# Reordering the start of an attention and feed-forward kernel: V of the first batch loaded after Q and K, and both heads of a pair normalised in one pass

## The chip, the cores and the metric

The kernel runs on one core of one Trainium2 chip. The metric is device time in microseconds (us) of that core; lower is better. Each kernel is executed several times in rounds that alternate with the kernel before. All numbers below are medians, and the profiles are of single executions, so a profiled span can differ from a median. Every run lists the granted clock of TensorE as a share of full speed. A run is labelled fast or slow; for one core, slow means over 1.5% above the fastest run of the same kernel.

A ratio in this document is the mean time of one kernel's fast runs over the mean of the other kernel's fast runs in the same rounds, with a 95% interval. It is therefore not quite the ratio of the medians that I quote beside it.

## The reference

There are 8 batches of 8 heads, 576 positions by 64. Blocks of 64 positions attend to themselves and to what lies before them. The result is laid out as 4608 rows of 512 and goes through a feed-forward layer. The shapes matter: every input is float32 in DRAM, and the kernel works in bf16.

```python
def _attn_ref(q, k, v):                      # 8 x 8 x 576 x 64
    scores = np.matmul(q, k.transpose(0, 1, 3, 2)) / np.sqrt(D)
    mask = (pos[:, None] // 64) >= (pos[None, :] // 64)
    scores = np.where(mask, scores, -1e9)
    ...                                      # softmax over the last axis
    return np.matmul(attn, v)

def _moe_ref(x, w_in, w_out, beta):          # x 4608x512, w_in 512x2048, w_out 2048x512
    h = x @ w_in
    g = h * (1.0 / (1.0 + np.exp(-beta * h)))
    return g @ w_out
```

## The kernel before

A unit is one pair of heads of one batch: four units to a batch, 32 in all. A unit loads Q and K, casts and transposes them, multiplies the scores in four groups, takes the exponentials on ScalarE (ACT), multiplies by V (with a column of ones, which gives the sum of each row), divides by that sum on VectorE (DVE), and transposes the result into xT. The feed-forward layer multiplies xT by w_in, applies its activation (the result is gT) and multiplies gT by w_out. It works on row chunks of 512 rows. Chunk 0 needs batch 0, and chunk 1 needs batch 1.

The program records operations with estimated durations in a plan. A list scheduler then fixes the order of every engine when the kernel is built. Each engine runs its list strictly in that order, and semaphores make it wait where an operand is not there yet. So an operation with a late operand also holds up those behind it on its engine. That property matters below.

The parts that the argument touches are the loads, and what each waits for. Q, K and most V loads are issued by the sync engine (SP), the first half of batch 0's V by ACT, and the weights by GpSimd (POOL):

```python
for a in range(4):                                   # w_in in four pieces of 512 columns
    win.append(P.op("POOL", 1000, fwi, xfer=4200, dma=(f"d_win{a}", 1), prio=-19))
for a in range(4):                                   # w_out likewise
    wout.append(P.op("POOL", 1000, fwo, xfer=4200, dma=(f"d_wout{a}", 1), prio=-18))
...
vs.append(P.op("ACT" if (b, h0) == (0, 0) else "SP", ...))   # loads of V
...
for w in win:
    w.deps += [ld["Q", 1], ld["K", 1]]
for w in wout:
    w.deps += [ld["Q", 6], ld["K", 6]]
for u in range(4, 8):                                # batch 1 waits for the second piece of w_in
    for o in [ld["Q", u], ld["K", u]] + (ld["V", 1, 0] if u == 4 else []):
        o.deps += [win[1]]
```

In PSUM, the memory into which TensorE writes its results, used here as eight banks, score groups take a pair of banks out of (0,1) and (2,3). Everything else, the V product too, takes single banks, mostly from 4 to 7. Two such banks serve one V product, and each head is normalised by itself:

```python
pa, pb = P.tile("P1"), P.tile("P1")
...
for w, p in enumerate((pa, pb)):                     # head 0, head 1
    r = P.op("DVE", 180, fr, deps=[av], tiles=[p, ti], prio=0)               # reciprocal, 128x5
    m = P.op("DVE", dve_t(320), fm, deps=[av, r], tiles=[p, ti, tx], prio=0) # multiply, 128x320
```

Finally there are fillers: multiplies of two constant matrices that nobody reads, which the scheduler puts where TensorE has nothing to do at the start, to keep its clock up.

The softmax here doesn't subtract the row's maximum and nothing guards it: scores larger than these inputs give would overflow.

Of the kernel before, what the change touches and what calls it, by code (L numbers as in the profile page):

```python
# [21 lines left out]
class Tile:  # L22


    def __init__(self, cls):
        self.cls, self.slot, self.left, self.users = cls, None, 0, []

# [16 lines left out]
class Plan:  # L44
# [29 lines left out]
    def schedule(self):  # L74
# [23 lines left out]
        def can(o):  # L98
            nb = {}
            for t in o.tiles:  # L100
                if t.slot is None:
                    nb[t.cls] = nb.get(t.cls, 0) + 1
            for c, n in nb.items():
                if c == "PP":
                    if sum(1 for a in (0, 2) if a in banks and a + 1 in banks) < n:
                        return False
                elif c == "P1":
                    ok = [k for k in banks if k >= 4 or pairs == 0]
                    if len(ok) < n:
                        return False  # L110
                elif len(free[c]) < n:
                    return False
            return True

        fill = [o for o in self.ops if o.fill]
        while nsched < len(self.ops) - len(fill) or pend:
# [25 lines left out]
            while progress:  # L142
                progress = False
                for e in engs:
# [4 lines left out]
                    for o in pool:  # L149
# [10 lines left out]
                        if o.fill and (now > o.fill or mode == "row"):  # L160
                            continue
# [16 lines left out]
                    for t in o.tiles:  # L178
                        if t.slot is None:
                            if t.cls == "PP":  # L180
                                a = next(a for a in (0, 2) if a in banks and a + 1 in banks)
                                banks.remove(a)
                                banks.remove(a + 1)
                                t.slot = a
                                o.deps += bank_last[a] + bank_last[a + 1]
                                pairs -= 1
                            elif t.cls == "P1":
                                ok = [k for k in banks if k >= 4 or pairs == 0]
                                t.slot = ok[0]
                                banks.remove(t.slot)  # L190
                                o.deps += bank_last[t.slot]
                            else:
                                t.slot = free[t.cls].pop(0)
                                o.deps += last[(t.cls, t.slot)]
# [90 lines left out]
def bass_blockwise_causal_attn__then__act_swish_beta_kernel(  # L285
# [10 lines left out]
    with es:  # L296
# [29 lines left out]
        ost = [sb(f"ost{i}", [128, DM], f32) for i in range(3)]  # L326
        PS = es.enter_context(nc.psum_tensor("PS", [128, 8, 512], f32))
# [19 lines left out]
        def pr(u):  # L347
            b, c = divmod(u, NPAIR)
            return 10 * u if b < 2 else 994 + 100 * (b - LAG) + 4.9 * c
# [12 lines left out]
        c2.same, c4.same = [c1], [c3]  # L362
        ones, vzero = [], []
# [11 lines left out]
        for i in range(NQ, NE):  # L375
# [12 lines left out]
        szero = [P.op("POOL", 350, mk(lambda g, i=i: g.memset(ST[i][64:128, 4, :, :], 0.0)), prio=-3)  # L388
                 for i in range(NS)]
# [3 lines left out]
        for a in range(4):  # L393
            def fwi(g, e, a=a):
                n = slice(512 * a, 512 * a + 512)
                return [g.dma_start(w_in[:, :, n], moe_w_in[:, n].rearrange("(c p) n -> p c n", p=128))]

            win.append(P.op("POOL", 1000, fwi, xfer=4200, dma=(f"d_win{a}", 1), prio=-19))
        for a in range(4):
            def fwo(g, e, a=a):  # L400
                return [g.dma_start(w_out[:, 4 * a:4 * a + 4, :],
                                    moe_w_out[512 * a:512 * a + 512, :].rearrange("(j p) n -> p j n", p=128))]

            wout.append(P.op("POOL", 1000, fwo, xfer=4200, dma=(f"d_wout{a}", 1), prio=-18))


        for i in range(NFILL):
# [5 lines left out]
            o = P.op("PE", 110, ff, deps=[c2, c4], tiles=[tf], lat=280, mode="full", prio=1e6)  # L413
# [5 lines left out]
        for b in range(B):  # L419
            ts, t = P.tile("Vs"), P.tile("V")  # L420
            tl[b] = t
            for h0, h1 in ([(0, 4), (4, 8)] if b == 0 else [(0, 8)]):
                vs = []
                for i in range(6):
                    def fv(g, e, ts=ts, b=b, h0=h0, h1=h1, i=i):
                        if i < 4:
# [7 lines left out]
                    vs.append(P.op("ACT" if (b, h0) == (0, 0) else "SP", 300 + 550 * n, fv, tiles=[ts],  # L434
                                   xfer=1400 * n, prio=(-50 if h0 == 0 else 3.5) if b == 0 else 4 * b + (3.5 if b < 2 else 0.5),
# [4 lines left out]
                def fw(g, e, ts=ts, t=t, h0=h0, h1=h1):  # L440
# [3 lines left out]
                         prio=4 * b + 0.5 - 30 * (b < 1))  # L444
                for h in range(h0, h1, 2):
                    load[4 * b + h // 2] = o

# [14 lines left out]
        for u in range(NU):  # L462
# [8 lines left out]
            if b < QB:  # L471

                turned = []
                for w, (nm, src) in enumerate((("Q", q), ("K", k))):
# [8 lines left out]
                    def fn(g, e, ts=ts, tn=tn, p=p, w=w):  # L483
# [3 lines left out]
                    onp = b == 1 or w == 1  # L487
                    o = P.op("POOL" if onp else "DVE", 850 if onp else 470, fn, deps=[o], tiles=[ts, tn],
                             prio=-26 + u if onp else -1)
# [14 lines left out]
                    turned.append(P.op("DVE", dve_t(576), fc, deps=[o], tiles=[pt, tt_], prio=0))  # L504
# [33 lines left out]
            for g0 in range(4):  # L538
# [17 lines left out]
                o = P.op("PE", 220 if g0 < 3 else 60, fq, deps=cps, tiles=[ps, tqk, te],  # L556
# [30 lines left out]
            pa, pb = P.tile("P1"), P.tile("P1")  # L587
            ti, tx = P.tile("inv"), P.tile("xq")

            def fav(g, e, te=te, pa=pa, pb=pb, Tv=Tv, c=c):  # L590
                for h in range(2):
                    for i in range(5):
                        for t in range(i + 1):
                            o = PS[:, (pa if h == 0 else pb).slot, 65 * i:65 * i + 65]
# [3 lines left out]

            av = P.op("PE", 30 * 34, fav, deps=ex + zs + [load[u]], tiles=[te, Tv, pa, pb, ti, tx],
                      lat=30 * 34 + 180, mode="full", prio=pr(u)+.4)  # L600
            nrm = []
            for w, p in enumerate((pa, pb)):
                def fr(g, e, w=w, p=p, ti=ti):
                    a = PS[:, p.slot, 0:325].rearrange("p (i n) -> p i n", n=65)[:, :, 64:65]
                    return g.reciprocal(inv[ti.slot][:, 5 * w:5 * w + 5].rearrange("p (i n) -> p i n", n=1), a)  # L605

                r = P.op("DVE", 180, fr, deps=[av], tiles=[p, ti], prio=0)

                def fm(g, e, w=w, p=p, ti=ti, tx=tx):
                    a = PS[:, p.slot, 0:325].rearrange("p (i n) -> p i n", n=65)[:, :, 0:64]  # L610
                    x = inv[ti.slot][:, 5 * w:5 * w + 5]
                    x = bass.AP(x.tensor, x.offset, [x.ap[0], [1, 5], [0, 64]])
                    return g.tensor_tensor(xq[tx.slot][:, :, 64 * w:64 * w + 64], a, x, ALU.mult)  # L613
                m = P.op("DVE", dve_t(320), fm, deps=[av, r], tiles=[p, ti, tx], prio=0)
                m.same = [r]
                nrm.append(m)
# [23 lines left out]
            xp = P.op("PE", 5 * 66, fx, deps=nrm, tiles=[tx, px], lat=5 * 66 + 170, mode="full", prio=pr(u)+.5)  # L640

            def fy(g, e, px=px, c=c, b=b):
                for t0, n, x0 in pieces(b):
                    z = g.tensor_copy(xT[:, c, x0:x0 + n], PSb[:, px.slot, t0:t0 + n])  # L644
                return z
            xt.append(P.op("DVE", 425, fy, deps=[xp], tiles=[px], prio=0))

        for w in win:
            w.deps += [ld["Q", 1], ld["K", 1]]
# [7 lines left out]
        for b in range(B):  # L657
            for u in range(4 * b, 4 * b + 4):
# [3 lines left out]
                if u == 4 * b + (3 if b < 2 else 1):  # L662
                    seq += ld["V", b, 4 if b == 0 else 0]
        for x, y in zip(seq, seq[1:]):
            y.after = x
        for o in seq:
            o.lazy = o not in seq[:28]
# [133 lines left out]
```

## Time and profile before

| before | |
|---|---|
| median (range, runs) | 366.44 us (365.94 to 368.33, 4) |
| granted TensorE clock | 1.00 in the profiled run; 0.99 to 1.00 in 134 runs of later rounds |
| first exponential | 12.52 us |
| last K of batch 0 landed | 15.46 |
| first multiply by w_in (feed-forward starts) | 32.46 |
| all of batch 1's V landed | 51.05 |
| batch 1's first V product | 53.64 |
| second row chunk starts | 75.60 |
| from there to the end | 289.1 |

The page of the profile shows the span in 40 slices, 9.1 us each here. Each digit is a busy share in tenths, or for PEclk the granted clock. These three rows are from the kernel before:

```profile
PE   7979999999897998999999999999999999999986
PEclk9999999999999999999999999999999999999999
DMA  8999999999799789995188998670202002002002
```

TensorE (PE) is nearly full from the fourth slice on, its clock never falls, and the DMA engines are full for the first ten slices. The stretches, the GpSimd timeline and the TensorE timeline of this kernel are shown in the prediction.

### The profile page before, as it was taken

What the parts mean: (1) busy time and instruction counts of PE and PEld (TensorE: products, weight loads), DVE (VectorE), ACT (ScalarE), POOL (GpSimd) and SP (SyncE); (2) the same over time, 40 slices, a digit from 0 to 9 for tenths busy, and PEclk for the clock granted to TensorE, in tenths of its full rate; (3) what the DMA queues carried; (4) which work ended last, traced back from release to release, by engine and by line L of the source; (5) the groups of instructions that cost most, each with busy time, mean ns of one, the idle gap of its engine ahead of it and who ended that gap; (6) DMA issues with size and microseconds to landing.
All of it is one profiled execution on the core that took longest, in us unless ns stands there. A gap on an engine that the chain in (4) does not pass through costs nothing.

```text
span 364.7 us, 6938 instructions
## 1 busy us (share of the span) xinstructions
PE 346.0 (95%) x2797; PEld 174.3 (48%) x2797; DVE 169.7 (47%) x437; ACT 209.2 (57%) x309; POOL 74.4 (20%) x102
## 2 busy tenths in 40 slices
PE   7979999999897998999999999999999999999986
PEld 5646445544444544554545434544544444444442
DVE  2675976146404764426854066307721721730800
ACT  1563794159438787539793499249733733833711
POOL 6714523241331251440005213200000000000000
PEclk9999999999999999999999999999999999999999
DMA  8999999999799789995188998670202002002002
GB/s 189 237 210 262 183 204 207 212 243 207 185 244 227 167 185 205 248 210 72 25 177 200 213 186 173 151 151 18 47 33 86 0 31 86 0 31 86 1 31 86
DMA packets 146528, 52.05 MB, mean 143 GB/s; under 512 B 134704, under 2 KB 141888, under 8 KB 146496
## 3 DMA queue, kind: packets, MB, share of 16 engines
q1 hardware_dynamic: 134688, 37.38, 50.5%
q10 hardware_dynamic: 7584, 10.03, 8.3%
q0 software_dynamic: 4224, 4.19, 7.1%
q8 instruction: 22, 0.36, 0.5%
q14 instruction: 10, 0.08, 0.1%
HBM read 36.71 MB, written 9.44 MB: 127 GB/s over the span
## 4 chain that ended last, share of the span: by engine, by line
PE 74%; ACT 14%; DVE 3%; issue 1%
PE PS L711 34%; PE PS L680 28%; ACT E L560 8%; PE PS L595 6%; ACT th L690 5%; PE PS L552 3%; DVE gT L694 2%; PE PS L637 2%; ACT ost L722 1%; PE PS L411 1%; ACT E L572 1%; DVE xq L613 0%; DVE xT L644 0%; DVE inv L605 0%; PE PS L493 0%
## 5 line engine op out<-in xcount | busy, mean ns | idle before, releaser
L680 PE MATMUL PS<-xT,w_in 128*128 128x512 bf16 x576 | 132.4, 380 | 1.1 <-DVE xT L644 0.6
L694 DVE SCALAR_TENSOR_TENSOR gT<-th,PS 128x512 bf16<-128x512 f32 x144 | 97.4, 685 | 71.8 <-ACT th L690 71.6
L711 PE MATMUL PS<-w_out,gT 128*128 128x512 bf16 x576 | 128.0, 379 | 2.7 <-DVE gT L694 2.7
L690 ACT ACTIVATE th<-PS,beta 128x512 f32<-128x512 f32 x144 | 99.3, 710 | 32.8 <-PE PS L680 32.7
L560 ACT ACTIVATE E<-PS 128x1024 bf16<-128x1024 f32 x96 | 96.7, 1063 | 15.0 <-PE PS L552 14.8
L711 PEld LDWEIGHTS PS<-w_out,gT 128*128 128x128 bf16 x576 | 55.1, 98 | 68.5 <-DVE gT L694 3.5
L680 PEld LDWEIGHTS PS<-xT,w_in 128*128 128x128 bf16 x576 | 52.7, 98 | 65.1 <-DVE gT L694 2.1
L722 ACT ACTIVATE ost<-PS 128x512 f32<-128x512 f32 x36 | 21.5, 597 | 100.2 <-PE PS L711 100.2
L523 POOL CAST QKn<-ST 128x640 bf16<-128x640 f32 x48 | 34.6, 720 | 48.3 <-DMA ST<-in_k_dram 27.1
L552 PE MATMUL PS<-QKT 64*64 64x64 bf16 (+5 forms) x384 | 37.2, 281 | 3.8 <-ACT E L560 3.1
L441 POOL CAST Vn<-Vs 128x2560 bf16<-128x2560 f32 (+1 forms) x9 | 18.7, 2082 | 99.1 <-DMA Vs<-in_v_dram 99.1
L595 PE MATMUL PS<-Vn,E 128*128 128x65 bf16 x960 | 34.4, 193 | 2.6 <-DVE gT L694 2.0
L595 PEld LDWEIGHTS PS<-Vn,E 128*128 128x128 bf16 x960 | 31.5, 97 | 7.9 <-DVE gT L694 2.5
L613 DVE TENSOR_TENSOR xq<-PS,inv 128x320 bf16<-128x320 f32 x64 | 28.8, 484 | 0.3
L552 PEld LDWEIGHTS PS<-QKT 64*128 64x128 bf16 (+1 forms) x384 | 13.5, 95 | 29.3 <-issue 11.3
L566 DVE MEMSET E<- 64x64 uint32 x64 | 7.2, 112 | 33.3 <-ACT E L560 31.1
L644 DVE COPY xT<-PS 128x64 bf16<-128x64 bf16 (+2 forms) x44 | 10.7, 288 | 21.1 <-PE PS L637 20.8
L605 DVE RECIPROCAL inv<-PS 128x5 f32<-128x5 f32 x64 | 8.7, 174 | 23.1 <-PE PS L595 22.8
L411 PE MATMUL PS<-identF,identB 128*128 128x256 bf16 x104 | 15.5, 306 | 2.2 <-POOL identF L355 2.2
L501 DVE COPY QKT<-PS 128x576 bf16<-128x576 bf16 x16 | 11.9, 751 | 5.9 <-PE PS L493 5.7
L568 DVE MEMSET E<- 64x128 uint32 x32 | 5.3, 165 | 18.5 <-ACT E L560 17.3
L411 PEld LDWEIGHTS PS<-identF,identB 128*128 128x128 bf16 x104 | 10.7, 110 | 5.0 <-POOL identF L355 2.2
(28 smaller groups left out, 63.9 us busy)
## 6 DMA issues: line engine op xcount, KB each, us to landing
out_dram<-ost ACTq DMA_DIRECT2D x36, 256.0 KB, 2.4
Vs<-in_v_dram SPq DMA_DIRECT2D x28, 256.0 KB, 4.0
ST<-in_q_dram SPq DMA_DIRECT2D x48, 128.0 KB, 2.9
ST<-in_k_dram SPq DMA_DIRECT2D x48, 128.0 KB, 3.2
ST<-in_q_dram SPq DMA_DIRECT2D x8, 288.0 KB, 7.6
ST<-in_k_dram SPq DMA_DIRECT2D x8, 288.0 KB, 7.8
w_in<-in_moe_w_in_dram POOLq DMA_DIRECT2D x4, 512.0 KB, 12.1
w_out<-in_moe_w_out_dram POOLq DMA_DIRECT2D x4, 512.0 KB, 9.8
```

The source lines that it names most:

```text
L411: return g.matmul(PS[:, tf.slot, 0:256], identB[:], identW)
L441: return g.tensor_copy(Vn[t.slot][:, :, h0:h1, 0:64], Vs[ts.slot][:, :, h0:h1, :])
L523: return g.tensor_copy(QKn[tn.slot][:].rearrange("p a w n -> p (a w n)")[:, 640 * (2 * a + w):][:, 0:640] .rearrange("p (t h d) -> p t h d ...
L552: z = g.matmul(o, QKT[tqk.slot][r, p, 1, 128 * t:128 * t + m], QKT[tqk.slot][r, p, 0, q0:q1])
L560: return g.activation(E3[te.slot][:, g0, :, :], PS[:, ps.slot:ps.slot + 2, :], ACT.Exp, scale=0.125)
L595: z = g.matmul(o, eblk(te, t, i, h), Vn[Tv.slot][:, t, 2 * c + h, 0:65], start=(t == 0), stop=(t == i))
L613: return g.tensor_tensor(xq[tx.slot][:, :, 64 * w:64 * w + 64], a, x, ALU.mult)
L680: z = g.matmul(PS[:, ph.slot, :], w_in[:, c, 128 * j:128 * j + 128], xT[:, c, row % RX:row % RX + RC], start=(c == 0), stop=(c == 3))
L690: return g.activation(th[tt.slot][:], PS[:, ph.slot, :], ACT.Tanh, scale=beta[:, j:j + 1])
L694: return g.scalar_tensor_tensor(out=gT[tg.slot][:, j, :], in0=th[tt.slot][:], scalar=1.0, in1=PS[:, ph.slot, :], op0=ALU.add, op1=ALU.mult)
L711: z = g.matmul(PS[:, po.slot, :], gT[tg.slot][:, j, 128 * w:128 * w + 128], w_out[:, j, :], start=(j == 0), stop=(j == NJ - 1))
L722: return g.activation(ost[to.slot][:], PS[:, po.slot, :], ACT.Copy, scale=0.5)
```

## The change

The intent is to start batch 0 sooner. Only Q and K should be loaded at first, and V after them. Six clears of pads (2.42 us on GpSimd) should no longer stand before the first casts. The last three pieces of w_in wait for V's second half, so that they do not take bandwidth from it. Also, the V product takes a bank pair, so that one reciprocal and one multiply normalise both heads. Fillers are used more sparingly, and some priorities and estimates change. The core of the diff, with cuts marked:

```diff
-                    vs.append(P.op("ACT" if (b, h0) == (0, 0) else "SP", 300 + 550 * n, fv, tiles=[ts],
-                                   xfer=1400 * n, prio=(-50 if h0 == 0 else 3.5) if b == 0 else 4 * b + (3.5 if b < 2 else 0.5),
+                    vs.append(P.op("SP", 300 + 550 * n, fv, tiles=[ts],
+                                   xfer=1400 * n, prio=3.5 + 0.1 * (h0 > 0) if b == 0 else 4 * b + (3.5 if b < 2 else 0.5),
 ...
-        szero = [P.op("POOL", 350, mk(lambda g, i=i: g.memset(ST[i][64:128, 4, :, :], 0.0)), prio=-3)
+        szero = [P.op("POOL", 420, mk(lambda g, i=i: g.memset(ST[i][64:128, 4, :, :], 0.0)), deps=[load[2]], prio=-3)
 ...
-                        if o.fill and (now > o.fill or mode == "row"):
+                        if o.fill and (now > o.fill or mode == "row" or sum(k >= 4 for k in banks) < 3):
 ...
-            pa, pb = P.tile("P1"), P.tile("P1")
+            pv = P.tile("PP")
+            pv.at = (4, 6, 0, 2) if u == 3 else (4, 6) if b < 1 else (0, 2)
 ...
+            r = P.op("DVE", 150, fr, deps=[av], tiles=[pv, ti], prio=0)
 ...
+            m = P.op("DVE", dve_t(640), fm, deps=[av, r], tiles=[pv, ti, tx], prio=0)
 ...
-        for w in win:
-            w.deps += [ld["Q", 1], ld["K", 1]]
+        for i, w in enumerate(win):
+            w.deps += [ld["Q", 3], ld["K", 3]] + (ld["V", 0, 4] if i else [])
```

Not shown: a dummy exponential that loads ACT's table early, the copy of two units' xT on ACT in place of DVE, the casts of two units' Q on GpSimd in place of DVE, lower priority for batch 0's V products, another choice among the single banks, and the estimate of a weight transfer (4200 to 3400). The rule that batch 1's loads wait for the second piece of w_in is not touched.

## The prediction

> **What bounds the kernel now.** I began with the page's busy shares: PE is at 95% and no other engine above 57%, but PE's row also counts filler multiplies (L411) that only keep it warm, so the share hides the start. So I took busy time by stretch, cut at the first input multiply of the feed-forward (L680, 32.46), at batch 1's first multiply by V (53.6), at the second row chunk (75.6), and at the end of attention (265.6). Columns: stretch, length, busy us of PE, weight load, DVE, ACT, POOL, clock, DMA share[...], GB/s.
>
> ```profile
> 0.00:32.46 32.46, 27.05 (x342) 19.70 (x343) 17.70 (x53) 13.17 (x17) 15.75 (x37) 1.00 1.10 223
> 32.46:53.60 21.14, 20.46 (x150) 9.35 (x147) 16.22 (x30) 17.13 (x26) 10.12 (x11) 1.00 1.17 200
> 53.60:75.60 22.00, 20.62 (x220) 11.63 (x217) 8.12 (x31) 6.76 (x10) 6.64 (x7) 1.00 1.00 220
> 75.60:265.60 190.00, 183.46 (x1657) 91.13 (x1658) 95.39 (x277) 131.09 (x195) 41.85 (x47) 1.00 0.78 166
> 265.60:364.70 99.10, 94.41 (x437) 42.47 (x435) 32.24 (x47) 41.08 (x62) 0.00 (x0) 1.00 0.12 43
> ```
>
> From 75.6 on PE is filled as well as this kernel can: 11 us of gaps in 289 by the last two rows (6.5 + 4.7). What can be won quickly lies before. There DMA is saturated (share 1.0 to 1.17), and of PE's 27 us before 32.46 the fillers are 15.5 (group of L411). So batch 0 is short of data. The timeline of GpSimd shows which data (start, length, instruction, idle time and what ended it):
>
> ```profile
> 4.45 2.42 POOL L388 MEMSET ST<- 64x256 f32 x6
> 7.02 0.82 POOL L484 CAST QKn<-ST 96x768 bf16<-96x768 f32 x1
> 10.52 0.82 POOL L484 CAST QKn<-ST 96x768 bf16<-96x768 f32 x1 [2.68 <-DMA ST<-in_k_dram]
> ...
> 23.75 1.25 POOL L441 CAST Vn<-Vs 128x1280 bf16<-128x1280 f32 x1 [5.60 <-DMA Vs<-in_v_dram]
> ...
> 51.11 2.32 POOL L441 CAST Vn<-Vs 128x2560 bf16<-128x2560 f32 x1 [9.28 <-DMA Vs<-in_v_dram]
> ```
>
> The first K block landed at 6.1 and its cast stood behind the clearing of pads (L388). The second half of batch 0's V is cast only at 23.75, and the third product with V starts at 25.15. The last line matters most to me: all of batch 1's V is cast at 51.11 to 53.43, after 9.28 us of waiting for the load. TensorE's timeline shows what follows it at once:
>
> ```profile
> 25.15 1.06 PE L595 MATMUL PS<-Vn,E 128*128 128x65 bf16 x30 [0.58 <-POOL Vn L441]
> ...
> 32.46 7.93 PE L680 MATMUL PS<-xT,w_in 128*128 128x512 bf16 x36
> ...
> 53.64 1.08 PE L595 MATMUL PS<-Vn,E 128*128 128x65 bf16 x30
> 55.46 1.08 PE L595 MATMUL PS<-Vn,E 128*128 128x65 bf16 x30 [0.74 <-DVE gT L694]
> ```
>
> Batch 1's first V product begins 0.2 us after that cast. In both programs every input multiply of row chunk 0 stands before it and nearly every output multiply (L711) behind it. So in the kernel before, the arrival of V for batch 1 is already about to bind.
>
> **What the Trainium skill says.** Three places. (1) DMA: Bandwidth & Descriptors, "Queues, rings and completion order": each engine goes round its queue rows packet by packet. The trace agrees: from 17 to 22 us, while w_in flows from GpSimd's queue, the sync queue moves about 145 packets a us of 256 B (V rows) beside some 153 of 1,024 B. One for one, V gets a fifth of the bytes; alone it moves 567 to 749 a us (at 15 and 37 us). So V beside weights is slow, and moving V ahead of the weights is the sound part of the change. (2) VectorE: DVE Perf Modes, "Why PSUM operands drop a tier": fp32 from PSUM runs at one element a cycle. The trace agrees: 128x320 takes 484 ns, of which 320/0.96 = 333 is elements and 151 fixed. (3) ScalarE: Activation LUTs, "What ACT_TABLE_LOAD costs": about 1283 ns; here one load of 1.28 us, from 4.84 to 6.12.
>
> **The change, part by part.**
>
> Start. Only Q and K (8 x 295 KB = 2.36 MB) now flow first; with V interleaved they took to 15.46. Packets start at 2.0; at the 260 GB/s of the stretch where Q and K flow alone (30 to 33 us), 2.36 MB ends at 11.1, and with the 1.1 us from last packet to landing the last K lands at about 12.2: 3.2 us sooner. The cleared pads (2.42 us on GpSimd) leave the path, so K's first cast starts at about 5.3 instead of 7.02. Fillers ahead of the first transposes fall from 38 to 18 (38 took 6.74, so 18 take 3.2), those between from 11 + 11 to 1 + 5: at 124 ns each 2 us off the way. My sum for the first exponential: K cast 6.1, second transposes and beta by 6.6, copy 7.4, next pair's transposes, scores: about 8.2 against 12.52. The table load needs no dummy to hide: it ended 6.4 us before its first use, though with a start at 8 it would be close.
>
> ACT has 12 exponentials of 1.02 and 4 of 0.23 = 13.2 us, near 12.9 overlapped; from 8.2 with about 0.7 us of gaps they end at 21.8 (before: 27.85). V follows: two halves of 2,304 packets at 750 a us are 3.1 us each, so first half 15.1, second 18.2 if undisturbed. But the first w_in piece is issued after the last K cast at 13.1 and flows 2.5 to 4.3 us after issue (as the first piece of w_out and of w_in did), so I put the second half at 19.7, its cast at 20.9. The last V product then runs at 23 to 24, normalisation 1.0, transposes 0.5, ACT's copy 0.8: first L680 at about 26, against 32.46. **6.4 us sooner.**
>
> Normalisation. Two reciprocals and two multiplies (0.26 + 0.89 us pipelined) become one of each: 0.17 + (640/0.96 + 151 = 0.82). 0.16 us a pair, 32 pairs, 5 us of DVE; but DVE is 47% busy. On the path it counts once, in batch 0's last pair. Nothing in steady state.
>
> What takes the 6.4 back. The pieces 2 to 4 of w_in now wait for V's second half, and stand behind its cast: issue at 21, flow at 23.4. Between 20 and 23.4 the DMA engines have nothing: **3.4 us idle** in a stretch that was saturated. Batch 1's loads wait for the second w_in piece, which landed at 23.36 and would now land at 23.4 + 2.6 + 1.2 = 27.2; they then flow at 29.5 rather than 26.3. Some of that returns, since the wait of 38.5 to 39.5 for descriptors may shrink: I take +2.5 us. V of batch 1 lands at 51.05 + 2.5 = 53.5, cast ends 55.9. TensorE, starting at 26, has 13.8 us of L680 and some 9 of transposes and scores ahead of that product, and ACT has 13 tanh, then 9 exponentials and 3 tanh, so TensorE is there at about 49 and waits 7 us. Then: first V product 55.9 (53.64 before), the second behind it without the 1.8 us pitch of before, ends 57.9 against 56.5, and the same 19 us of work to chunk 1: 76.7 against 75.6. **Net to there: +1 us**, from -3 (V at 50) to +4.
>
> Steady state. From batch 1 on, the V product takes a bank pair out of the two that scores use. By pairs, a unit holds 3 x (0.35 + 1.02 + 0.3) + (0.95 + 0.97 + 0.3) = 7.2 pair-us, over two pairs 3.6 us, against 3.2 us of exponentials: where attention units come in close succession, the pairs are now the tighter limit, 0.4 us each for perhaps ten units, +4 at most. Against it four banks stay free for the feed-forward, which waited 4.2 us for DVE's gT (PE's waits between 32.4 and 270), and the new order of TensorE mixes scores more evenly with L680. I take -2 with 2.5 either way.
>
> Sum: 366.6 + 1.1 - 2 = 365.7; since a re-tuned order seldom is left in when it loses, I lean 0.7 us down: 365.0.
>
> **Rivals.** (A) The 6.4 us survive: V of batch 1 comes by 49, because without V of batch 0 beside them the weights finish sooner. Against it: DMA share 1.17 up to 53.6, and 3.4 us of idle added. It would make 358 to 360. (B) The weights become the bound: chunk 0 needs w_in's second to fourth piece at +3.45, +6.9, +10.4 us from 26, i.e. 29.5, 32.9, 36.4; I have them at 27.2, 30.5, and 33 to 36 once batch 1's Q and K (1,536 B packets, one for one, 60% of bytes) share. The fourth is close: a stall here costs nothing more while V is waited for later. Time about 366. (C) Bank pairs cost more than 4 us: ACT idle with exponentials waiting for scores behind a V product; 369 to 372. It speaks against it that the order was laid by the same scheduler knowing the pairs.
>
> **Range and chances.** Front part -3 to +4 and steady state -4.5 to +2, partly cancelling: 359.8 to 370.5 for 8 in 10. Faster by over 2% means under 359.3, rival A whole or most of it with a good steady state: 0.12. Slower by over 2% means over 374: 0.03. Within: 0.85.
>
> **What would show it.** Right: first exponential near 8, first L680 near 26, an empty DMA slice near 20 to 23, batch 1's V cast ending at 55 to 57, and several us of PE idle before its first V product, released by that cast; second chunk within 2 us of 75.6. Wrong: V of batch 1 cast before 52 (then the gain at the start is kept), no idle before that product, or a first L680 later than 29. Steady state is read from the second chunk's start to the end: 289.1 us before; I expect 286 to 290, and more than 291 with ACT waiting for scores would be rival C.

## The result, and the profile after

| | before | after |
|---|---|---|
| median (range, runs) | 366.44 (365.94 to 368.33, 4) | 376.13 (375.41 to 380.57, 4) |
| ratio, 95% interval | | 1.029 (1.021 to 1.037): slower |
| granted clock | 1.00 (profiled run) | 0.963 to 0.977 (six runs) |
| first exponential | 12.52 | 8.93 |
| last K of batch 0 landed | 15.46 | 12.34 |
| second half of batch 0's V landed | 23.70 | 21.75 |
| second piece of w_in landed | 23.36 | 29.38 |
| first multiply by w_in | 32.46 | 28.18 |
| last K of batch 1 landed | 38.65 | 44.02 |
| all of batch 1's V landed | 51.05 | 60.42 |
| batch 1's first V product | 53.64 | 62.84 |
| second row chunk starts | 75.60 | 85.38 |

All listed runs are labelled fast, and both results are correct. The change is 2.9% slower, and I had 365.0 with a range to 370.5. The prediction was wrong.

First, the same three rows of the page, from the kernel after (slices of 9.5 us):

```profile
PE   7779923999899799999999999999999999999986
PEclk9899985999999689999999999999999999999999
DMA  8969999989989987699066899870121002001002
```

There are two things to see. PE has a hole in the sixth and seventh slices (47 to 66 us) while DMA stays at 9, so TensorE waits for transfers that are under way. And PEclk, which was 9 everywhere, is lower right there, in the second slice (half clock from 16.0 to 19.4 us) and again near 130 us. DMA also has a dip to 6 in the third slice.

Next, busy time by stretch in the kernel after, cut at the same events as in the prediction, with the wait of TensorE as a stretch of its own. The columns are stretch, length, busy us of PE, weight load, DVE, ACT, POOL, then clock, DMA share (the times of all packets over that of 16 engines, so it can pass 1), GB/s:

```profile
0.00:28.18 28.18, 21.10 (x272) 13.83 (x272) 14.75 (x39) 14.59 (x22) 15.50 (x38) 0.94 0.85 167
28.18:49.67 21.49, 20.43 (x148) 9.52 (x148) 16.62 (x30) 17.39 (x27) 9.48 (x12) 1.00 1.19 228
49.67:62.84 13.17, 0.01 (x2) 0.00 (x0) 0.96 (x3) 1.96 (x3) 2.32 (x1) 0.65 1.10 193
62.84:85.38 22.54, 22.54 (x217) 13.11 (x217) 6.60 (x19) 4.98 (x7) 8.10 (x9) 0.90 0.90 199
85.38:279.80 194.42, 187.41 (x1658) 92.87 (x1657) 91.91 (x229) 131.58 (x194) 40.51 (x45) 0.97 0.75 159
279.80:378.80 99.00, 94.29 (x437) 42.37 (x434) 32.36 (x47) 41.84 (x63) 0.00 (x0) 1.00 0.12 44
```

The feed-forward starts 4.3 us sooner. TensorE is through with all it can do at 49.67 and then does nothing for 13.17 us. That is where the gain went, and 9 us more. TensorE's timeline in the kernel after names the releaser:

```profile
28.18 9.67 PE L695 MATMUL PS<-xT,w_in 128*128 128x512 bf16 x44 [0.15 <-ACT xT L657]
...
62.84 3.48 PE L605 MATMUL PS<-Vn,E 128*128 128x65 bf16 x60 [13.17 <-POOL Vn L447]
```

L447 is the cast of V on GpSimd. The GpSimd timeline of the kernel after shows why that cast is late (start, length, instruction, idle time before it and what ended that):

```profile
14.74 1.25 POOL L447 CAST Vn<-Vs 128x1280 bf16<-128x1280 f32 x1 [0.70 <-DMA Vs<-in_v_dram]
21.80 1.26 POOL L447 CAST Vn<-Vs 128x1280 bf16<-128x1280 f32 x1 [5.81 <-DMA Vs<-in_v_dram]
23.00 2.23 POOL L401 DMA_DIRECT2D w_in<-in_moe_w_in_dram  x3
...
44.91 2.23 POOL L406 DMA_DIRECT2D w_out<-in_moe_w_out_dram  x3
60.47 2.32 POOL L447 CAST Vn<-Vs 128x2560 bf16<-128x2560 f32 x1 [13.33 <-DMA Vs<-in_v_dram]
```

Three pieces of w_in are issued at 23.00, behind the cast of V's second half (before: 11.29, in the cast queue's first gap). Their first packet flows at 24.45; the last one of V had flowed at 21.28. For these 3.2 us the DMA engines move nothing. The same two microseconds in both kernels, in the columns of the stretches, first the kernel before:

```profile
22.00:24.00 2.00, 1.92 (x39) 1.27 (x38) 1.43 (x7) 2.00 (x5) 0.25 (x1) 1.00 1.25 207
```

and the kernel after:

```profile
22.00:24.00 2.00, 0.80 (x27) 0.83 (x28) 0.65 (x3) 0.15 (x1) 2.00 (x3) 1.00 0.00 0
```

The DMA share is 1.25 before and 0.00 after. The second piece of w_in lands at 29.38. SP, which had been held for it, issues batch 1's first load at 29.39, and those packets flow from about 32.4. The last K of batch 1 lands at 44.02, which is 5.4 us later than before. From there to V's landing it takes 16.4 us, against 12.4 before, so V lands 5.4 + 4.0 = 9.4 us later.

In most of those last 16 us V shares with w_out. From 54 to 58 us, counted in windows of 2 us, the trace has 143 to 145 packets a us of 256 B, which are rows of V, and 155 to 158 of 1,024 B, which are w_out. That is about one for one, so V gets a fifth of the bytes. The kernel before shares in the same way (147 to 152 beside 151 to 154 from 47 to 51 us), so the sharing alone does not explain the 4.0 us by which the distance grew.

What follows the wait is slowed as well. The granted clock is half from 53.6 to 67.2 us, that is for 13.7 us, of which the last 4.4 fall on work: the two V products that come first take 3.48 us.

In the profiled run, the second row chunk starts 9.8 us later than before, and the rest takes 293.4 us against 289.1. But the profiled run is one of the two longest (378.8 us of span) and has a third stretch of half clock, 125.3 to 135.5. The other four listed runs have spans of 373.6 to 374.6. If their second chunk starts at 85.4 too, which only a profile of them would show, they need about 289 us from there, as before.

### The profile page after: what moved, and what is told of

The parts are those of the page before. It is cut to its first block, busy times and chain, and to the rows that moved or that the text cites. A ratio compares the mean times of both kernels' runs of the same rounds, so it can differ in the third digit from the quotient of the medians.

```text
span 378.8 us, 6727 instructions
## 1 busy us (share of the span) xinstructions
PE 345.8 (91%) x2728; PEld 171.7 (45%) x2728; DVE 163.2 (43%) x367; ACT 212.3 (56%) x314; POOL 75.9 (20%) x105
## 4 chain that ended last, share of the span: by engine, by line
PE 64%; SPq 7%; ACT 6%; DMA 3%; DVE 2%; issue 1%
PE PS L726 28%; PE PS L695 25%; PE PS L605 6%; SPq L521 4%; PE PS L561 4%; ACT E L569 3%; SPq L637 2%; ACT th L705 2%; DMA QKT<-QKn 2%; PE PS L649 2%; DVE gT L709 1%; DMA xT<-xq 1%; SPq L524 1%; SPq L436 0%; DVE xq L624 0%
## 5 line engine op out<-in xcount | busy, mean ns | idle before, releaser
L569 ACT ACTIVATE E<-PS 128x1024 bf16<-128x1024 f32 x96 | 95.8, 1044 | 20.0 <-PE PS L561 19.7
L605 PE MATMUL PS<-Vn,E 128*128 128x65 bf16 x960 | 37.9, 201 | 16.2 <-POOL Vn L447 14.9
L561 PE MATMUL PS<-QKT 64*128 64x512 bf16 (+5 forms) x384 | 40.6, 290 | 7.5 <-ACT E L569 5.5
L605 PEld LDWEIGHTS PS<-Vn,E 128*128 128x128 bf16 x960 | 35.7, 103 | 23.7 <-POOL Vn L447 13.4
L447 POOL CAST Vn<-Vs 128x2560 bf16<-128x2560 f32 (+1 forms) x9 | 18.8, 2084 | 105.9 <-DMA Vs<-in_v_dram 105.9
L561 PEld LDWEIGHTS PS<-QKT 64*128 64x128 bf16 (+1 forms) x384 | 13.7, 96 | 31.1 <-issue 9.7
L624 DVE TENSOR_TENSOR xq<-PS,inv 128x640 bf16<-128x640 f32 x32 | 26.3, 822 | 0.9
L617 DVE RECIPROCAL inv<-PS 128x10 f32<-128x10 f32 x32 | 7.0, 219 | 44.5 <-PE PS L605 44.3
L659 DVE COPY xT<-PS 128x64 bf16<-128x64 bf16 (+2 forms) x40 | 9.6, 286 | 15.9 <-PE PS L649 15.8
L581 ACT ACTIVATE E<-PS 128x64 bf16<-128x64 f32 x32 | 7.0, 251 | 16.5 <-PE PS L561 14.9
L493 POOL CAST QKn<-ST 96x768 bf16<-96x768 f32 x14 | 11.6, 827 | 13.7 <-DMA ST<-in_q_dram 10.2
```

Of the source, the lines that this page charges most:

```text
L447: return g.tensor_copy(Vn[t.slot][:, :, h0:h1, 0:64], Vs[ts.slot][:, :, h0:h1, :])
L561: z = g.matmul(o, QKT[tqk.slot][r, p, 1, 128 * t:128 * t + m], QKT[tqk.slot][r, p, 0, q0:q1])
L569: return g.activation(E3[te.slot][:, g0, :, :], PS[:, ps.slot:ps.slot + 2, :], ACT.Exp, scale=0.125)
L605: z = g.matmul(o, eblk(te, t, i, h), Vn[Tv.slot][:, t, 2 * c + h, 0:65], start=(t == 0), stop=(t == i))
L624: return g.tensor_tensor(xq[tx.slot][:].rearrange("p i (h d) -> p h i d", h=2), both(pv, 0, 64), x, ALU.mult)
```

## The experiments

Fourteen kernels ran, and all gave correct results. Names that begin with b_ are built on the kernel before, the others on the kernel after. If nothing else is said, an edit stands after the call that lays the order, so the order of all other engines stays as it was. The diffs are shortened to the lines that matter, and `last_QK_cast_before_load4` in one of them stands for a longer expression. The theories: **hold** (w_in held, so batch 1's loads wait longer), **sharing** (w_out takes bandwidth from batch 1's V), **pairs** (the bank pair or the joint normalisation costs), and **clock** (fewer fillers let TensorE's clock fall).

| run | median us (range, runs) | ratio (95%) | batch 1's V landed | its first product | second chunk |
|---|---|---|---|---|---|
| a_nogate | 372.21 (369.67 to 373.06, 4) | 1.014 (1.009 to 1.019) | 54.52 | 56.95 | 80.08 |
| a_woutlate | 371.90 (370.99 to 375.41, 4) | 1.016 (1.010 to 1.022) | 48.28 | 52.15 | 78.98 |
| a_both | 369.42 (363.68 to 372.41, 20) | 0.998 (0.995 to 1.001) | 43.70 | 55.82 | 76.43 |
| b_hold | 372.73 (371.54 to 373.30, 4) | 1.016 (1.012 to 1.020) | 54.47 | 56.89 | 79.33 |
| b_pair | 367.41 (365.55 to 368.29, 20) | 1.002 (1.000 to 1.003) | 48.78 | 53.46 | 74.58 |
| a_p1 | 376.88 (375.36 to 380.69, 4) | 1.030 (1.023 to 1.036) | 59.22 | 61.65 | 85.36 |
| a_fill | 377.21 (376.95 to 381.93, 5) | 1.028 (1.026 to 1.031) | 60.80 | 65.00 | 85.61 |
| b_fewfill | 367.34 (366.82 to 369.31, 18) | 1.003 (1.002 to 1.004) | 51.64 | 54.07 | 75.12 |
| a_best | 369.99 (365.35 to 374.63, 20) | 1.006 (1.003 to 1.008) | 45.81 | 53.23 | 75.47 |
| a_best_fill | 370.73 (367.62 to 372.44, 4) | 1.010 (1.005 to 1.016) | 45.10 | 53.23 | 75.23 |
| a_p1_best | 368.76 (365.87 to 372.38, 20) | 1.004 (1.001 to 1.007) | 43.75 | 51.46 | 73.39 |
| a_p1_best_fill | 367.46 (365.13 to 371.24, 20) | 1.002 (1.000 to 1.004) | 44.44 | 50.02 | 74.71 |
| bestA | 366.64 (364.68 to 368.70, 14) | 1.000 (0.998 to 1.003) | 48.33 | 50.75 | 73.05 |
| bestB | 370.07 (369.04 to 371.81, 6) | 1.009 (1.006 to 1.012) | 53.13 | 55.55 | 78.23 |

The three columns on the right are of one profiled execution each. They are the better evidence for where time goes; the ratio says whether it counts.

### The hold and the sharing

**b_hold** puts the hold alone into the kernel before: the last three pieces of w_in go behind the cast of V's second half and wait for that half.

```diff
+        pool[:] = [o for o in pool if o not in win[1:]]
+        at = pool.index(load[2]) + 1            # load[2] is the cast of V's second half
+        pool[at:at] = win[1:]
+        for o in win[1:]:
+            o.deps += ld["V", 0, 4]
```

> The kernel before with one thing of the change alone: w_in's pieces 2 to 4 wait for V's second half of batch 0 and stand behind its cast on GpSimd. Order otherwise as before. Theory 1: DMA idle for some 3 us near 21 to 24, batch 1's V lands at 57 to 60 instead of 51.05, PE idle of 3 to 6 us before its V product, second chunk at 80 to 84 instead of 75.6, time 371 to 375. Rival (the hold is harmless, the loss comes from the other parts): time 365 to 368.

It measured 372.73, some 6 us over the kernel before. GpSimd's timeline of this run:

```profile
21.53 2.23 POOL L396 DMA_DIRECT2D w_in<-in_moe_w_in_dram  x3
...
54.52 2.32 POOL L441 CAST Vn<-Vs 128x2560 bf16<-128x2560 f32 x1 [9.49 <-DMA Vs<-in_v_dram]
```

and TensorE's:

```profile
56.89 3.37 PE L595 MATMUL PS<-Vn,E 128*128 128x65 bf16 x60 [4.27 <-POOL Vn L441]
```

In a kernel that otherwise is the one before, the hold makes an idle DMA (8 GB/s from 20.0 to 23.5), a later second piece of w_in (27.09 against 23.36), a later last K (41.58 against 38.65), a later V (54.47), a wait of 4.27 us that was not there, and half clock right after the wait. The second chunk comes 3.7 us later. So the hold by itself loses time, but less V delay (3.4 us) than the whole change (9.4 us).

**a_nogate** takes out of the kernel after the rule that batch 1's loads wait for the second piece of w_in.

```diff
+        for o in ld["V",1,0] + [ld[w,u] for w in "QK" for u in range(4,8)]:
+            o.deps = [d for d in o.deps if d is not win[1]]
```

> The changed kernel with the same order on every engine; batch 1's Q, K and V loads no longer wait for w_in's second piece. Theory 1 (the added time is batch 1's V landing late: 60.42 us against 51.05, because its load is behind an idle DMA stretch near 22-24 us and behind the weights): the loads fill that stretch, V of batch 1 lands at 49 to 52, its first V product starts near 52 to 54 instead of 62.8, second row chunk at 74 to 76 instead of 85.4, time 364 to 368, PE idle before that product under 5 us. Rival 2 (V is late because it shares the DMA engines with w_out, whatever the gate): V lands at 57 or later, time 372 to 376. Rival 3 (the steady state with the bank pairs loses the 10 us): second chunk earlier, but from there to the end over 293 us and time not below 372.

**a_woutlate** issues w_out only behind the cast of batch 1's V, and makes it wait for that.

```diff
+        pool[:] = [o for o in pool[:at+1] if o not in wout] + wout + [o for o in pool[at+1:] if o not in wout]
+        for o in wout:                          # at: place of load[4], the cast of batch 1's V
+            o.deps += [load[4]]
```

> The changed kernel, only w_out's four pieces are moved behind batch 1's V cast on GpSimd's queue. Theory 1: the gate on w_in still holds K and Q of batch 1 back (last K lands at 44), but V then flows alone and lands near 48 instead of 60.4; V product at 50; w_out lands 56 to 65, which costs some 4 us of waits before the output multiplies; second chunk near 75 to 77, time 364 to 368. Rival 2 (V's lateness comes from sharing with w_out and nothing else): the same V at 48. If w_out late is dear instead: V at 48 but second chunk at 80 or later, time over 371. Rival 3: time not below 372.

a_nogate won 3.9 us of the 9.7, with V landing 5.9 us sooner. Its TensorE timeline still has a wait of half the size for the same releaser:

```profile
56.95 3.48 PE L605 MATMUL PS<-Vn,E 128*128 128x65 bf16 x60 [6.67 <-POOL Vn L447]
```

a_woutlate won 4.2 us, with V landing 12.1 us sooner, 5.4 us after the last K. Without w_out beside it, V moves some 780 to 800 packets a us between 42 and 46 us. On TensorE two other waits took the place of the one removed:

```profile
52.15 2.65 PE L605 MATMUL PS<-Vn,E 128*128 128x65 bf16 x60 [2.10 <-ACT E L569]
...
58.60 1.49 PE L726 MATMUL PS<-w_out,gT 128*128 128x512 bf16 x3 [3.62 <-DMA w_out<-in_moe_w_out_dram]
```

The V product now waits for an exponential, since V is there, and the first multiply by w_out, 6.5 us behind it, waits for its weights. The clock is half from 53.2 to 63.4 in this run. So V gains what w_out loses: both are wanted between 50 and 58 us.

**a_both** is both edits together.

> Both edits together. Theory 1: V of batch 1 lands near 43, TensorE reaches its first V product at about 49 and does not wait for it; w_out lands 51 to 60; second chunk at 69 to 72, time 359 to 363, that is under the kernel before by 1 to 2%: the start's gain is then kept. Rival 3 (steady state): time 366 or more although the second chunk starts by 72.

Its 20 runs spread over 8.7 us, and 11 of them were labelled slow because they lie over 1.5% above the fastest. The ratio of 0.998 counts only the nine fastest, so it flatters this kernel, whose median over all runs is 369.42. I read it as inconclusive. In its profile V landed at 43.70, but batch 1's early loads shared with batch 0's V and w_in: V's second half landed at 24.10 (21.75 in the kernel after), the third V product waited 2.69 us, and the feed-forward started only at 32.45. The clock was half from 16.4 to 30.0 as well, and how much of the delay is due to that is not separated. The lead was gone before it could be lost.

### The pairs

**b_pair** gives the kernel before the bank pair, with one reciprocal and one multiply, from batch 1 on. **a_p1** gives the kernel after the old single banks and two passes from batch 1 on. Both are planned anew by the scheduler, so their order differs in places.

```diff
-            pa, pb = P.tile("P1"), P.tile("P1")
+            pv = P.tile("PP")                   # b_pair: if b >= 1;  a_p1: the other way round
```

> The kernel before with the bank pair and the one-pass normalisation from batch 1 on and nothing else of the change (planned anew; the order up to batch 1's V products is the same as before). The prediction's claim (steady state between -4.5 and +2 us): second chunk at 75 to 77, from there to the end 285 to 291 us, time 363 to 369. Rival 3 (the bank pair makes V products and scores wait for each other; TensorE's short idle stretches then bring half-clock stretches after the second chunk): half clock in the records where the kernel before has none, waits of V products for ACT's E or of scores for DVE's xq, time 368 to 373.

> The changed kernel with single banks and the two-pass normalisation from batch 1 on, batch 0 as changed (planned anew; order the same up to batch 1's first V product). Theory 1: V of batch 1 lands at 60 as in the changed kernel, second chunk at 83 to 86; if the bank pair is harmless the time stays 374 to 377; if it costs (rival 3), 368 to 373.

b_pair came to 1.002 (1.000 to 1.003), which is at most 1.1 us of 366. a_p1 came to 376.88, no better than the kernel after, and its TensorE timeline has the same stall:

```profile
61.65 3.48 PE L639 MATMUL PS<-Vn,E 128*128 128x65 bf16 x60 [11.95 <-POOL Vn L447]
```

From batch 1 on, the pairs are not the cause; batch 0's pairs were not tested by themselves. Where V comes early they do cost something at one place: in a_woutlate, a_both, a_best and a_best_fill the first V product of batch 1 stands 2.10 us before an exponential of the unit that holds the pair, and in a_p1_best and a_p1_best_fill, with single banks, that wait is absent.

### The clock

**a_fill** puts 100 fillers, into the bank of batch 1's first V product, ahead of that product in the kernel after.

```diff
+        pe.insert(pe.index(avs[4]), filler(100))   # multiplies of constants, 128x256, where TensorE would wait
```

> The changed kernel with 100 filler multiplies put on TensorE's queue just ahead of batch 1's first V product, where it stands idle for 13.2 us; they run into the bank that this product will overwrite. Nothing else moves. If the idle stretch also costs by leaving TensorE at half clock afterwards (13.7 us of half clock in the changed kernel's profile, two V products in 3.5 us instead of 2.0): full clock there, second chunk some 2 us earlier at 83.4, time 373 to 375 against 376.1. If the clock is only a symptom: 376. V of batch 1 lands at 60 either way, so most of the loss must stay.

The clock stayed full after the wait. TensorE's timeline of a_fill, which answers to the line at 62.84 of the kernel after:

```profile
65.00 1.97 PE L610 MATMUL PS<-Vn,E 128*128 128x65 bf16 x60
```

The two V products took 1.97 us, not 3.48, and from there to the second chunk it was 20.6 us, not 22.5: so the half clock behind the stall costs 1.9 us. But I had put in too many. They ran to 65.1, about 2 us after V's cast had ended at 63.2, and ate what they won: the second chunk starts at 85.61. As a time it is a miss (377.21), and as a measurement of the clock's share it served.

**b_fewfill** cuts the fillers of the kernel before from 104 to 71, at the places where the change has few.

```diff
+        ...                                        # runs: the groups of fillers in TensorE's list
+        keep = [38, 11, 11, 0, 0, 0, 0, 6, 5]      # of groups of 38, 11, 11, 5, 11, 5, 1, 14, 8
+        gone = [o for r, n in zip(runs, keep) for o in r[n:]]
+        pe[:] = [o for o in pe if o not in gone]
```

> The kernel before with the filler multiplies between the first scores and the first L680 cut to the changed kernel's number (5, 11, 5, 1, 14, 8 become 0, 0, 0, 0, 6, 5); order otherwise the same. If the fillers keep the clock up through batch 0: half-clock stretches appear between 13 and 33 us, the first L680 comes 0 to 4 us later than 32.46, time 367 to 371. If they do nothing but fill: full clock, time 366 to 367.

It had one stretch of half clock of 3.4 us, at 16.3, where the kernel before has none, and took 1.003 (1.002 to 1.004). So fewer fillers lowered the clock, and that alone is worth about 1 us here.

### Looking for a version that keeps the gain

**a_best** issues all of w_in right behind the cast of V's first half, not waiting for the second, and w_out behind the cast of batch 1's V.

```diff
+        after(load[0], win, [])                    # load[0]: cast of the first half of batch 0's V
+        after(load[4], wout, [load[4]])            # load[4]: cast of batch 1's V
```

> The changed kernel with GpSimd's queue reordered: the four w_in pieces directly behind the cast of V's first half and waiting for nothing of V's second half; the four w_out pieces behind batch 1's V cast. Batch 1's loads still wait for w_in's second piece. Theory 1: V's second half lands at 18.5 to 21, first L680 at 25 to 28, w_in's second piece lands near 25, batch 1's V near 43 to 45, no wait for it (TensorE gets there at 47 to 50), second chunk at 68 to 73, time 358 to 364 at full clock, 2 to 6 us more with half-clock stretches. If V of batch 1 is early and the time is still 368 or more at a clock over 0.99, theory 1 is not the whole.

**a_best_fill** adds fillers: three ahead of each score group and V product of batch 0, eight ahead of its third and fourth product.

> The same as a_best with 3 fillers ahead of each score group and V product of batch 0 (8 ahead of the third and fourth V product). If half-clock stretches in batch 0 are what spreads the times: none before 33 us, time 357 to 362, spread under 1%. If not: the same times as a_best.

**a_p1_best** is a_p1 with the edit of a_best. **a_p1_best_fill** adds 22 fillers to that, two ahead of some score groups and six ahead of the third V product.

> The same with GpSimd's queue reordered as in a_best. Both causes removed: V of batch 1 near 45, its first V product at 50 to 52 without the 2.1 us wait for the second bank of the pair, second chunk at 71 to 74, clock over 0.985, time 360 to 364. If it is 366 or more with V at 45, a cause is still missing.

> The same with 22 fillers in batch 0 (2 ahead of some score groups, 6 ahead of the third V product). If half clock in batch 0 is left in a_p1_best: it goes, and the time falls by 0 to 3 us, to 358 to 363, with less spread. If not: the same as a_p1_best.

In a_best V landed at 45.81, and the second chunk started at 75.47, 9.9 us before that of the kernel after and level with the kernel before. The time of 369.99 is nevertheless above: its clock was 0.974 in the median, with half clock for 13.7 us from 9.4 and 10.2 us from 115 in its profile. The fillers of a_best_fill shortened that to 3.4 us in its profile. But some of them stood ahead of scores that were already wanted (the first V product came at 19.32, not 17.31), and its median was no better. a_best and a_woutlate have w_out in the same place and differ only in where w_in stands and what it waits for, so this pair too shows the hold: in a_woutlate, which has it, V lands 2.5 us and the second chunk starts 3.5 us later.

The single banks in a_p1_best brought the second chunk to 73.39, 2.2 us ahead of the kernel before. In a_p1_best_fill, V was no longer waited for, but w_out was:

```profile
54.91 1.40 PE L765 MATMUL PS<-w_out,gT 128*128 128x512 bf16 x4 [1.60 <-DMA w_out<-in_moe_w_out_dram]
```

**bestA** is a_p1_best_fill with the first piece of w_out issued before the cast of batch 1's V and the other three behind it. **bestB** is bestA with all four pieces of w_in behind the cast of V's second half.

```diff
-        after(load[4], wout, [load[4]])
+        after(load[4], wout[1:], [load[4]])
+        after(last_QK_cast_before_load4, wout[:1], [])
-        after(load[0], win, [])                    # bestB alone
+        after(load[2], win, [])                    # bestB alone: cast of the second half
```

> a_p1_best_fill with w_out's first piece issued ahead of batch 1's V cast instead of behind it. If the wait for w_out and the half clock behind it eat the gain: no wait before the first output multiply, no half clock near 55, second chunk at 70 to 72.5 instead of 74.7, time 362 to 365 median. If the later part is to blame: second chunk by 72.5 and the time still 366 or more at a clock over 0.99.

> bestA with w_in's pieces behind the cast of batch 0's second V half too. V's second half then lands by 20 (22.2 in a_p1_best_fill), first L680 at 26.5 to 28.5, but w_in's first piece lands only at 26 to 27.5 and batch 1's V 2 to 3 us later than in bestA, near 47; second chunk within 1 us of bestA's, time 362 to 366. If the DMA engines' idle stretch near 21 to 23 costs as in the changed kernel: 366 or more.

bestA has both transfers nearly in time. Its TensorE timeline:

```profile
50.75 1.98 PE L645 MATMUL PS<-Vn,E 128*128 128x65 bf16 x60 [0.97 <-POOL Vn L449]
...
73.05 3.19 PE L734 MATMUL PS<-xT,w_in 128*128 128x512 bf16 x14 [0.62 <-DVE xT L698]
```

The second chunk starts at 73.05, 2.5 us before that of the kernel before; this is what was left of the 4.3 us. From there the run takes 291.0 us, against 289.1, with 6.8 us of half clock at 113.5 inside. It ends level: 1.000 (0.998 to 1.003). bestB, whose only difference is where w_in is issued, has V at 53.13 and this wait:

```profile
55.55 3.48 PE L645 MATMUL PS<-Vn,E 128*128 128x65 bf16 x60 [6.24 <-POOL Vn L449]
```

Its ratio is 1.009. This is the cleanest statement of the hold: one place in one queue is worth 0.9%. No version is faster than the kernel before.

The profiles also say what half clock costs once the second chunk has started. From there to the end, the eight profiles without it (but for the last 1 us of the run) take 288.8 to 290.7 us; the two with 3.4 us of it 291.0 and 291.2; the three with 6.8 us 291.0 to 293.5; the two with 10.2 us 293.3 and 293.4; the one with 13.7 us 294.5. A straight line through all sixteen rises by about 0.3 us for each us of half clock. This goes across different kernels, so it is a tendency and no test.

## Why the prediction was wrong

**What held.** The kind of mechanism was as predicted. The first exponential came at 8.93 (I had 8.2), the last K at 12.34 (12.2), TensorE stood before batch 1's first V product from 49.67 on (49), and the wait was ended by the cast of V. The DMA engines were empty for 3.2 us up to 24.45 (3.4, up to 23.4). The feed-forward started at 28.18 (26): V's second half came 2 us later than I had it. The joint multiply takes what I worked out, 0.82, and the joint reciprocal somewhat more, 0.22 against 0.17. The group of the multiply in the kernel before, and then in the kernel after:

```profile
L613 DVE TENSOR_TENSOR xq<-PS,inv 128x320 bf16<-128x320 f32 x64 | 28.8, 484 | 0.3
```

```profile
L624 DVE TENSOR_TENSOR xq<-PS,inv 128x640 bf16<-128x640 f32 x32 | 26.3, 822 | 0.9
```

320 more elements cost 338 ns, as I had it with 333. Rival C fell with b_pair and a_p1. Rival A, that the gain survives, fell with the result. Rival B does not show: between 28.18 and 49.67 TensorE is idle for only 1.06 us.

**The step that failed.** It is the sentence "I take +2.5 us. V of batch 1 lands at 53.5", and with it "**Net to there: +1 us**, from -3 (V at 50) to +4". V landed at 60.42, and the second chunk came 9.8 us late. The sign of this front part was right, and its size was off in three terms, which add up to the 6.9 us by which V came later than I said (2.2 + 0.7 + 4.0).

1. The second piece of w_in came 6.0 us later (29.38), where I had 3.8 (27.2), that is 2.2 more, mostly because V's second half landed at 21.75 and not at 19.7: the first w_in piece flows from 15.01, beside it. b_hold shows the kind (3.7 us later in that kernel), and bestA against bestB what it costs.
2. I let part of the delay come back ("Some of that returns"). Nearly nothing did: 5.4 of the 6.0 us are still there at the last K of batch 1, where I had let 1.3 of 3.8 go: 0.7 more. The removal of the rule in a_nogate brought V 5.9 us forward.
3. I left the distance from the last K to V as it was. It grew from 12.4 to 16.4 us, 4.0 more. I had the one-for-one sharing in the prediction, but did not follow it to batch 1's V, where w_out takes part; a_woutlate shows that without w_out the distance is 5.4 us. But w_out was in the 12.4 us too, so what made the distance grow is not shown.

So V lands at 60.42 and not at 53.5, and its first product comes 6.9 us later as well (62.84 against 55.9). The half clock after the wait, which I had not in the sum at all, adds 1.7 up to the second chunk (22.5 us against my 20.8; a_fill measured its cost at 1.9). Together this is the 8.7 us between 85.4 and my 76.7. The rest of the 11.1 us between 376.1 and 365.0, some 2.4, is the -2 that I gave the steady state and the 0.7 that I leaned down, less 0.3 of small differences: by the spans of the other runs the steady state is about even.

Three readings in the prediction were off without deciding anything. The packets of the kernel before flow 1.45 us (w_out, 37.20 to 38.65) and 3.9 us (w_in) after their issue, not 2.5 to 4.3. The 567 packets a us at 15 us were not V alone: 77 of weights flowed beside them. And 57.9 with the 19.1 us of the kernel before makes 77.0, not 76.7.

**The lean was a fault of its own.** "A re-tuned order seldom is left in when it loses" is no reading of a profile, and the profile said otherwise: a chain that bound within 0.2 us in the kernel before was going to be delayed by two named causes.

**Why mending it gives nothing over the kernel before.** With V early, 0.1 to 2.5 us of the 4.3 reach the second chunk in a_best to bestA. One reason that the traces show is w_out: in bestA its first multiply starts 2.6 us behind the first V product, and its weights come by the same engines. The other is the clock: all variants of the kernel after have a median granted clock of 0.97 to 0.995, where the kernel before has 1.00. That a lower clock goes with a longer time shows in the runs of the kernel after: its two longest, 379.98 and 380.57, have the two lowest clocks, 0.964 and 0.963. I did not separate what the clock alone is worth in bestA by an experiment. But its four runs at a clock of 1.00 took 364.7 to 366.1, 365.6 in the mean, and the sixteen such runs of the kernel before in the same rounds 366.6. So about 1 us of the lead seems to last where the clock is not lowered.

**What stays open.** Why V needed 16.4 us from the last K in the kernel after, and 12.9 in b_hold, with the same queues in the same order: from 50 to 54 us the trace of the kernel after counts only 65 to 88 packets a us of 256 B beside 171 to 184 of w_out, so not even one for one, and the last of V's six loads landed 3.7 us after the one before it (1.7 in the kernel before, 1.8 in b_hold). No run tells why. And whether a_both is faster at an undisturbed clock: its fast runs at clock 0.99 or above reach 363.7 to 365.5, but one at 0.99 takes 368.6.

## What to carry to other kernels

When a change holds back one transfer to favour another, follow what waits for the held one through to the next batch: here a hold of w_in moved loads that only its semaphore tied to it, and V came 9.4 us later, 5.4 of them already in the last K before it. With the 4.3 us that TensorE had won before, that made a wait of 13 us. If a load already ends within a fraction of a microsecond of binding, its delay must be worked out term by term, sharing included, before any gain upstream is counted. A stall can also cost after it has ended: here the waits of 13.17 and 4.27 us were followed by half clock.

## What the Trainium skill lacked or had wrong

- **TensorE: Matmul & The Clock Gate, "HAM oscillation — how this bites in real kernels"**: its rule in brief is "no PE-idle gaps >~3.4µs" (HAM is the page's name for the monitor that sets the clock). In the runs here that was not sufficient. In the kernel after, the clock was half from 16.03 to 19.44, and from 8 us up to there no gap of TensorE was above 0.53 us. The two windows, in the columns of the stretches, with the clock in third place from the end:

```profile
12.60:16.03 3.43, 2.27 (x29) 0.97 (x25) 2.76 (x7) 3.43 (x6) 2.70 (x3) 1.00 0.90 143
16.03:19.44 3.41, 2.97 (x40) 1.91 (x36) 0.50 (x4) 1.86 (x4) 0.00 (x0) 0.50 1.16 181
```

  The window before the fall was busy for 2.27 us of 3.43. In a_woutlate one with 2.78 of 3.41 busy was followed by half clock too. So busy shares of 66 and 82% did not keep the clock up. Nor does a low share always bring it down: in the kernel after, the window from 19.44 to 22.85 was busy for 1.99 us, 58%, and the clock stayed full. The page speaks further on of short idle times that come often, but gives no share, and what decides is not shown here. In b_fewfill, with 33 fillers fewer than the kernel before, half clock appeared.
- **The same page, "Part 1: The HAM clock gate"**: that the throttle is half and that its window is 3413 ns agrees. The stretches of half clock were 3.4, 6.8, 10.2 and 13.7 us long, one to four windows. They also come in the middle of a busy kernel, such as that at 125.3 to 135.5 in one run of the kernel after: TensorE was busy for 9.0 of 10.2 us inside it, and for 2.08 of 3.42 us just before.
- **DMA: Bandwidth & Descriptors, "Queues, rings and completion order"**: it says that an engine drains a packet of about 9 to 17 descriptors from one ring before it switches. What these traces count as packets are single rows, 256 B of V and 1,024 B of weights, and these flow about one for one (143 to 145 and 155 to 158 a us), so V's short rows got a fifth of the bytes. That the share here went by row and not by bytes the page does not say. From 50 to 54 us even one for one was not kept (65 to 88 against 171 to 184).
- **The same page, the table at its head**: it gives about 1 us to the first byte for loads issued by GpSimd. Here the first packet of a weight load flowed 1.45 us after its issue where nothing else was under way (issue at 23.00, packet at 24.45), 1.8 us beside the sync queue's loads, and 3.9 us in the kernel before (issue at 11.29, packet at 15.20).
